# Half-block issue rules and a move of late scaling and sums to VectorE in a fused attention and gated-unit kernel

## The chip, the cores and the metric

The kernel runs on one core of one Trainium2 chip. The metric is the device time of one launch in microseconds (us). The engines are named as the profile names them: PE is TensorE (matmuls; PEld are its weight loads), ACT is ScalarE, DVE is VectorE, POOL is GpSimd, and SP is the engine whose queue issues nearly all transfers.

## The reference

The input is a sequence of 2048 rows of 640 features. It is normalised over the features, and then goes through two branches: full attention with 32 heads of 20 features each, and a gated unit with 1728 hidden features. The result combines the two.

```
xn = layernorm(A_x)
q, k, v = split_heads(xn @ wqkv)              # 32 heads of 20
s = softmax(q k^T * 20**-0.5) v, heads joined, @ wo
g = silu((sigmoid(xn @ w_gate) * (xn @ w_up)) @ w_down)
out = A_x + s * g
```

All arrays are bf16. The exponentials dominate: 32 heads x 2048 x 2048 scores.

## The kernel before

**Blocks.** Attention is cut into 32 blocks: 8 groups of 4 heads times 4 chunks of 512 queries. A block has 64 score tiles (4 heads x 16 key tiles), each 128 keys x 512 queries, one PSUM bank. The last two groups are interleaved (blocks 24 to 31), so block 30 is the last but one, and 31 the last. `base()` is the first block with score tiles not yet claimed, and `n_left[b]` counts them.

**Two ways to an exponential.** A score tile goes either to ScalarE (line 144, `pu<-pst`, two to four banks in one instruction) or to VectorE, where line 1337 turns it to int16 (`iv`) and three passes over four tiles (lines 1040, 1043, 1046, `pb`) build the exponential from its bits. The score matmuls are line 936, and the sums over the keys (PV matmuls) line 988. When a block's PV is complete, `norm_a` copies the sums out (line 1002) and sends the row sums through DRAM, `norm_b` takes the reciprocal (line 1012) and spreads it back (`rl`), and `norm_c` multiplies (line 1025, GpSimd) and stores the scaled block in DRAM (`oD`). Block 30's scaled rows go to an SBUF tile instead (`o6`, line 1029; it appears as `o` in the profile), since the end of the kernel reads it at once.

**Work in between.** Projections and the gated unit (lines 578, 686, 718, 756) are lists of items that fill PE between score fills. `mk_out` items (lines 813 to 825) multiply a finished 128-row tile by `wo`, half a row at a time (h = 0, 1): VectorE multiplies by the gate (line 820) and GpSimd adds the input (line 823); the last sum of a tile is on VectorE once all scores are claimed. `mk_part` items (lines 843 to 851) do the same for the first part of the last four tiles.

**Order.** The order on each engine is written by a planner that runs while the kernel is built: a loop over a clock of 0.01 us which holds a duration for each operation and picks what PE, ACT and DVE issue next. On the chip an engine executes its instructions in that order and waits only for its inputs. The planner's choices are set by 23 numbers (`KEYS`), of which `PLAN` holds one row per block. The ones used below: `wait3` is how long PE waits for a further bank for a wider ScalarE instruction, `third` chooses the banks that may be so used, `four` allows two such banks, `s0` and `dmax` bound how many score tiles VectorE takes per fill, `dl` and `dle` are the numbers of tiles left in a block (`dle` in the last) below which VectorE takes no more, `lag` sets how far the items run ahead.

`gos` is the list of scalings that are ready to be issued: an entry is taken by VectorE's turn from a given time on, as soon as two score tiles wait for VectorE, or 8.0 us (`GO_WAIT`) later at the latest; for odd blocks from 24 (`pressing`) 1.5 us later. VectorE then writes one element (line 1023), which lets GpSimd's multiply start; `pool_at` and `pool_from` keep VectorE's passes in the plan clear of GpSimd. Block 30 was the exception: its multiply was put on GpSimd at once after `norm_b`, with no such signal.

**The end.** After the last PV of block 31 a chain of steps runs: `e_on` (ACT copy), `e_tr` (PE transpose, line 1089), `e_scale` (DVE, lines 786 and 788), `e_back` (PE, line 1098), `e_o` (ACT, line 1102). `early` (line 1076) multiplies `o6` by `wo`, `late_mm` (line 1080) adds block 31, and `tail_steps` combines and stores the last four tiles (lines 1122 to 1136).

Of the kernel before, what the change touches and what calls it, by code (L numbers as in the profile page):

```python
# [14 lines left out]
ALU = mybir.AluOpType  # L15
# [25 lines left out]
            dmax=2, third=4, dord=0, mord=0, mfew=2, npv=4, held=48, burst=1, excl=1, dl=20, dle=8, one=1, four=1, pair=0)  # L41
KEYS = tuple(RULE)
PLAN = (
    (0.25, 4, 0.15, 0.2, 1.8, 0.2, 0.2, 1, 0.0, 2, 4, 0, 5, 2, 3, 48, 1, 1, 20, 8, 1, 1, 0),
    (0.25, 4, 0.15, 0.2, 1.8, 0.2, 0.2, 1, 0.0, 2, 4, 4, 5, 2, 3, 48, 1, 1, 20, 8, 1, 1, 0),
    (0.25, 4, 0.15, 0.2, 1.8, 0.2, 0.2, 1, 0.0, 2, 4, 2, 5, 1, 3, 48, 1, 1, 20, 8, 1, 1, 0),
    (0.25, 5, 0.15, 0, 1.8, 0.2, 0.2, 1, -2.0, 2, 4, 2, 5, 1, 4, 48, 1, 1, 20, 8, 1, 1, 0),
    (0.25, 4, 0.15, 0.2, 1.8, 0.2, 0.2, 1, 0.0, 2, 4, 2, 3, 1, 3, 48, 1, 1, 20, 8, 1, 1, 0),
    (0.25, 5, 0.15, 0, 1.8, 0.2, 0.2, 1, -2.0, 2, 4, 2, 5, 1, 4, 48, 1, 1, 28, 8, 1, 1, 0),
    (0.25, 5, 0.15, 0, 1.8, 0.2, 0.2, 1, -2.0, 2, 4, 2, 3, 1, 4, 48, 0, 1, 20, 8, 1, 1, 0),  # L50
    (0.25, 5, 0.15, 0, 1.8, 0.2, 0.7, 1, 14.0, 2, 4, 2, 3, 1, 4, 48, 0, 1, 20, 8, 1, 1, 0),
    (0.25, 5, 0.15, 0, 0.8, 0.2, 1.0, 1, 14.0, 2, 4, 2, 3, 1, 4, 48, 0, 1, 20, 8, 1, 1, 0),
    (0.25, 4, 0.15, 0.2, 1.8, 0.2, 0.7, 1, 0.0, 2, 4, 0, 0, 2, 4, 48, 1, 1, 20, 8, 1, 1, 0),
    (0.25, 5, 0.15, 0, 0.8, 0.2, 1.0, 1, 14.0, 2, 4, 2, 3, 1, 4, 48, 0, 1, 20, 8, 1, 1, 0),
    (0.25, 5, 0.15, 0, 0.8, 0.2, 1.0, 1, 14.0, 2, 4, 2, 0, 1, 4, 48, 0, 1, 14, 8, 1, 1, 0),
    (0.25, 4, 0.15, 0.2, 1.8, 0.2, 0.7, 1, 0.0, 2, 4, 4, 0, 2, 4, 48, 1, 1, 20, 8, 1, 1, 0),
    (0.25, 5, 0.15, 0, 0.8, 0.2, 1.0, 1, 14.0, 2, 4, 2, 3, 1, 3, 52, 0, 1, 20, 8, 1, 1, 0),
    (0.25, 5, 0, 0, 0.8, 0.2, 1.0, 1, 14.0, 2, 4, 2, 3, 1, 3, 52, 0, 1, 20, 8, 1, 1, 0),
    (0.25, 2, 0.15, 0, 0.8, 0.2, 1.0, 1, 14.0, 2, 2, 2, 5, 1, 3, 52, 0, 1, 20, 8, 1, 1, 0),
    (0.25, 5, 0, 0, 0.8, 0.2, 1.0, 1, 14.0, 2, 3, 2, 3, 1, 3, 52, 0, 1, 20, 8, 1, 1, 0),  # L60
    (0.25, 5, 0, 0, 0.8, 0.2, 1.0, 1, 14.0, 2, 3, 2, 3, 1, 3, 52, 0, 1, 20, 8, 1, 1, 0),
    (0.45, 5, 0, 0, 0.8, 0.2, 1.0, 1, 14.0, 2, 1, 2, 3, 1, 3, 52, 0, 1, 20, 8, 1, 1, 0),
    (0.45, 5, 0, 0, 0.8, 0.2, 1.0, 1, 14.0, 2, 1, 2, 1, 1, 3, 52, 1, 1, 20, 8, 1, 1, 0),
    (0.25, 5, 0, 0, 0.8, 0.2, 1.0, 1, 14.0, 2, 3, 2, 3, 1, 3, 48, 0, 1, 20, 8, 1, 1, 0),
    (0.25, 5, 0, 0, 0.8, 0.2, 1.0, 1, 14.0, 2, 3, 2, 3, 1, 3, 48, 0, 1, 20, 8, 1, 0, 0),
    (0.25, 4, 0, 0, 0.8, 0.2, 1.0, 1, 14.0, 2, 3, 2, 3, 1, 3, 48, 0, 1, 28, 8, 1, 1, 0),
    (0.25, 4, 0, 0, 0.8, 0.2, 1.0, 1, 14.0, 2, 3, 2, 3, 1, 3, 48, 0, 1, 28, 8, 1, 1, 0),
    (0.25, 4, 0, 0, 0.8, 1.2, 1.0, 1, 14.0, 2, 3, 2, 3, 3, 3, 48, 0, 1, 28, 8, 1, 1, 0),
    (0.25, 4, 0, 0, 0.8, 0.2, 1.0, 1, 8.0, 2, 3, 2, 1, 1, 3, 48, 0, 1, 28, 8, 1, 1, 0),
    (0.25, 4, 0.3, 0, 0.8, 0.2, 1.0, 1, 8.0, 2, 3, 2, 1, 1, 3, 48, 0, 1, 28, 8, 1, 1, 0),  # L70
    (0.25, 4, 0, 0, 0.8, 1.2, 1.0, 1, 14.0, 2, 3, 2, 3, 3, 3, 48, 1, 1, 28, 8, 1, 1, 0),
    (0.1, 4, 0, 0, 0.8, 0.2, 1.0, 1, 8.0, 2, 3, 2, 1, 2, 4, 48, 0, 1, 28, 8, 1, 1, 0),
    (0.25, 4, 0.3, 0, 0.8, 1.8, 1.0, 1, 0.0, 2, 3, 2, 1, 2, 4, 48, 0, 1, 28, 8, 1, 1, 0),
    (0.25, 4, 0.3, 0, 0.8, 1.8, 1.0, 1, 0.0, 2, 3, 0, 1, 2, 4, 48, 0, 1, 28, 8, 1, 1, 1),
    (0.25, 4, 0.3, 0, 0.8, 1.8, 1.0, 1, 0.0, 2, 2, 2, 5, 2, 4, 32, 0, 1, 28, 10, 1, 1, 0),
)

PRO = (
# [35 lines left out]
def kernel(  # L114
# [389 lines left out]
    def mark(*e):  # L504
        return lambda t: ev_at.__setitem__(e, t)
# [286 lines left out]
    def load_out(tt):  # L792
# [5 lines left out]
        nc.sync.dma_start(out=out_tiles[tt][1], in_=gq_dram[tt * P:(tt + 1) * P, :])  # L798
        ev_at[("ol", tt)] = now + 4.0

    def pool_hold(t):
        pool_from[0] = max(pool_at[0], t)
        pool_at[0] = pool_from[0] + 0.82

    def mk_out(tt, h, at):
        st = {}

        def alloc():
            st["ps"] = misc_ps()

        def mm(kd):
            hs = slice(h * HD, (h + 1) * HD)
            nc.tensor.matmul(st["ps"][:, 0:HD], lhsT=o_mid[:, kd, tt % 4 * P:(tt % 4 + 1) * P], rhs=wo[kd][:, hs],  # L813
                             start=(kd == 0), stop=(kd == KD - 1))

        def ev():
            xr, gqr = out_tiles[tt]
            sl = slice(h * HD, (h + 1) * HD)
            tmp = w2.tile([P, HD], FP32, tag="gqs", bufs=3, name="otmp")
            nc.vector.scalar_tensor_tensor(out=tmp, in0=st["ps"][:, 0:HD], scalar=0.25,  # L820
                                           in1=gqr[:, sl], op0=ALU.mult, op1=ALU.mult)
            add = nc.vector if h == 1 and claimed[0] == NJOB * NBLK else nc.gpsimd
            add.tensor_tensor(out=xr[:, sl], in0=tmp, in1=xr[:, sl], op=ALU.add)  # L823
            if h == 1:
                nc.sync.dma_start(out=out2[tt * P:(tt + 1) * P, :], in_=xr)
        return Item([("PE", alloc, [(0.136, lambda kd=kd: mm(kd)) for kd in range(KD)]),
                     ("DVE", 0.40, ev, "free", lambda t: (mark("o", tt, h)(t), pool_hold(t)))], at, need=blk(NG - 1, tt // 4),
                    pre=[("oc", tt // 4), ("ol", tt)])


# [189 lines left out]
    def norm_c(b, on, rl, sync):  # L1020
        g, c = gc(b)
        if sync:
            nc.vector.memset(rl[0:1, 0:1], 1.0)  # L1023
        on_bf = w2.tile([P, QC], BF16, tag="on_bf", bufs=2, name="on_bf")
        nc.gpsimd.tensor_tensor(out=on_bf, in0=on, in1=rl, op=ALU.mult)  # L1025
        if b == NBLK - 2:
            last["o6"] = wk.tile([P, QC], BF16, tag="aq", bufs=4, name="o6")[0:GC, :]
            for j in range(GH):
                nc.sync.dma_start(out=last["o6"][j * DH:(j + 1) * DH, :], in_=on_bf[32 * j + 1:32 * j + 1 + DH, :])
            return  # L1030
        for j in range(GH):
            f = g * GC + j * DH
            nc.sync.dma_start(out=oD[f:f + DH, c * QC:(c + 1) * QC], in_=on_bf[32 * j + 1:32 * j + 1 + DH, :])
# [104 lines left out]
    with tc.manual_schedule(engines={ENG.PE, ENG.Activation, ENG.DVE}):  # L1138
# [16 lines left out]
        cur = None  # L1155
        mode = None
        rule = dict(RULE)
        blk_loaded = -1
        active = []
        u_next, k_next, q_next, k_at = 0, PG, PG * NQC, {}  # L1160
        o_next, l_next = 0, 0
# [38 lines left out]

        guard = 0
        chain_at = 1e9
        while chain or items or glu_items or any(it.i < len(it.ops) for it in active):
            guard += 1
            assert guard < 240000, "the issue order does not end"
            bb = base()
            if bb > blk_loaded:
                blk_loaded = bb
                rule.update(zip(KEYS, PLAN[bb]) if bb < len(PLAN) else ())
                g, c = gc(bb)  # L1210
                if c == 0 and g + 1 < NG:
                    if g % 2 == 1:
                        wvs[(g + 1) // 2] = load_wv((g + 1) // 2)
# [49 lines left out]
            for eng in ("ACT", "DVE"):  # L1263
# [15 lines left out]
                if eng == "DVE" and gos and gos[0][0] <= now and (  # L1279
                        sum(x[3] <= now + 0.3 for x in dq) >= 2 or now > gos[0][0] + (1.5 if pressing(gos[0][1]) else GO_WAIT)):  # L1280
                    _, b, on, rl = gos.pop(0)
                    norm_c(b, on, rl, True)
                    free["DVE"] = now + T_GO
                    pool_from[0] = max(pool_at[0], now + T_GO + 0.15)
                    pool_at[0] = pool_from[0] + 1.3
                    o_at[b] = pool_at[0] + 4.0
                    continue
                it = next((e for e in active if e.i < len(e.ops) and e.ops[e.i][0] == eng and e.open(now)), None)
                if it is not None:
                    op = run_item(it, eng)  # L1290
                    if len(op) > 3 and op[3] == "free":
                        flex[it.bank] = free[eng] + EL[eng]
                    continue
                if eng == "ACT":
                    s = slots[nexp % 2]
# [20 lines left out]
                if tm is not None:  # L1316
                    timed.remove(tm)
                    rl = norm_b(*tm[1:3], tm[3])
                    free["DVE"] = now + 0.16
                    if tm[1] == NBLK - 2:  # L1320
                        norm_c(tm[1], tm[2], rl, False)
                        o_at[tm[1]] = now + 11.5
                        ev_at[("o6",)] = now + 9.5
                    else:
                        gos.append((now + (7.0 if pressing(tm[1]) else GO_AT), tm[1], tm[2], rl))
                    continue
                iv_ok = dq and dq[0][3] <= now
                pass_ok = dve_pass and not (now < pool_at[0] and dq and dq[0][3] <= now + 0.2) and dve_pass[0].get("at", 0.0) <= now and (dve_pass[0]["k"] > 0 or buf_free(pb_left, NPB))
# [227 lines left out]
```

## Time and profile before

| | |
|---|---|
| median of 8 runs | 794.59 us (793.39 to 796.48) |
| the profiled execution | 795.5 us, span 793.8 us |
| granted TensorE clock, mean | 0.995 |
| first exponential of attention on ScalarE | 33.24 us after the start of the span |
| last score matmuls | in 774 to 777 us |
| moved by transfers | 62.62 MB, 79 GB/s |

A group line of the profile names the line, the engine, the operation, the tile written and the tiles read with their shapes, then `x` the count; behind the first bar the busy time in us and the mean length of one in ns; behind the second the idle time of the engine just before them and what ended it. ScalarE's instructions overlap in their records (a next one starts before the one before has ended), so the sum of their lengths is more than the busy time. A timeline line begins with start and length in us; x3 behind it means three instructions merged, and brackets hold the idle time before. In a table of windows the busy times are followed by the granted clock, the share of the transfer engines and GB/s.

### The profile page before, as it was taken

Reading aid. Unit: us, or ns where it says so; the run is one execution under the profiler, and the core shown is the slowest. Engines: PE = TensorE matmul, PEld = TensorE weight load, DVE = VectorE, ACT = ScalarE, POOL = GpSimd, SP = SyncE. Lnnn points to the kernel's source line nnn. Section 1 sums busy time; section 2 is a strip of 40 time slices with the busy share of each in tenths; the row PEclk is TensorE's granted clock in tenths of the full one; section 3 lists DMA queues with packets and bytes.
Section 4 is the critical chain, followed back from the end, with each engine's and each line's share of the span. In section 5 each row is a group of like instructions: output and inputs, shape, how many; then the busy total and the mean of one; then the engine's idle time right before and its main releaser. Section 6 shows DMA issues by size and latency. Waiting matters only on the chain.

```text
span 793.8 us, 17201 instructions
## 1 busy us (share of the span) xinstructions
PE 756.6 (95%) x6509; PEld 273.6 (34%) x6509; DVE 771.5 (97%) x1270; ACT 769.7 (97%) x846; POOL 90.5 (11%) x104
## 2 busy tenths in 40 slices
PE   7899999999999999999999999999999999999895
PEld 6532332333333233334333322333332323333332
DVE  8899999999999999999999999999999999999997
ACT  7899999999999999999999999999999999999992
POOL 6100000001000000000000000000000002302354
PEclk9999999999999999999999999999999999999998
DMA  6521221124222133312114333233123322422511
GB/s 169 160 64 48 69 62 49 46 58 102 69 80 66 33 84 102 86 53 56 48 50 112 96 82 81 61 92 114 41 81 92 90 59 66 117 73 84 160 35 64
DMA packets 95876, 62.62 MB, mean 79 GB/s; under 512 B 36388, under 2 KB 89684, under 8 KB 95792
## 3 DMA queue, kind: packets, MB, share of 16 engines
q1 hardware_dynamic: 95504, 61.18, 27.9%
q8 instruction: 51, 0.84, 0.4%
q14 instruction: 33, 0.27, 0.1%
q10 hardware_dynamic: 288, 0.33, 0.1%
HBM read 47.84 MB, written 13.55 MB: 77 GB/s over the span
## 4 chain that ended last, share of the span: by engine, by line
PE 43%; ACT 39%; DVE 10%; issue 5%; DMA 1%; SPq 1%; ACTq 0%; DVEq 0%
ACT pu L144 34%; PE pst L936 14%; PE pst L988 9%; PE pst L718 8%; PE pst L756 5%; PE pst L578 3%; ACT tnh L144 3%; DVE iv L1337 2%; DVE pb L1046 1%; PE pst L813 1%; ACT td L144 1%; DVE pb L1043 1%; DVE pb L1040 1%; DVE otmp L820 1%; SPq L266 1%
## 5 line engine op out<-in xcount | busy, mean ns | idle before, releaser
L144 ACT ACTIVATE pu<-pst 128x1024 bf16<-128x1024 f32 (+2 forms) x706 | 736.6, 1315 | 2.9 <-PE pst L936 2.8
L1337 DVE TENSOR_SCALAR iv<-pst 128x512 int16<-128x512 f32 x491 | 324.8, 682 | 5.0 <-PE pst L936 2.6
L936 PE MATMUL pst<-q,kT 32*128 32x512 bf16 x2048 | 269.0, 383 | 16.4 <-ACT pu L144 10.8
L988 PE MATMUL pst<-pu,v 128*21 128x512 bf16 x1556 | 175.6, 382 | 0.0
L936 PEld LDWEIGHTS <-kT 32*128 32x128 bf16 x2048 | 82.8, 91 | 257.3 <-issue 245.7
L988 PE MATMUL pst<-pb,v 128*21 128x512 bf16 x984 | 153.5, 382 | 1.7 <-DVE pb L1046 1.0
L1046 DVE TENSOR_TENSOR pb<-iv,pb 128x2048 bf16<-128x2048 bf16 x123 | 151.6, 1233 | 0.6
L718 PE MATMUL pst<-xnT,wgu 128*128 128x512 bf16 x520 | 145.6, 384 | 0.9 <-DVE bt L645 0.4
L1025 POOL TENSOR_TENSOR on_bf<-on,rl 128x512 bf16<-128x512 f32 x31 | 40.0, 1291 | 641.8 <-DVE rl L1023 544.8
L1040 DVE TENSOR_SCALAR pb<-iv 128x2048 int16<-128x2048 int16 x123 | 85.3, 694 | 0.1
L1043 DVE TENSOR_SCALAR pb<-iv 128x2048 int16<-128x2048 int16 x123 | 84.4, 686 | 0.0
L756 PE MATMUL pst<-wd,hT 128*128 128x320 bf16 x448 | 83.1, 302 | 0.9 <-DVE iv L1337 0.5
L988 PEld LDWEIGHTS <-v 128*21 128x21 bf16 x2540 | 48.7, 91 | 83.6 <-issue 61.3
L718 PEld LDWEIGHTS <-wgu 128*128 128x128 bf16 x520 | 38.5, 97 | 63.1 <-issue 41.4
L756 PEld LDWEIGHTS <-hT 128*128 128x128 bf16 x448 | 35.9, 97 | 39.7 <-issue 29.5
L144 ACT ACTIVATE tnh<-pst 128x512 bf16<-128x512 f32 (+1 forms) x56 | 45.8, 818 | 0.0
L578 PE MATMUL pst<-xnT,wu 128*128 128x512 bf16 x160 | 45.4, 383 | 0.4 <-DVE iv L1337 0.4
L726 DVE SCALAR_TENSOR_TENSOR hT<-tnh,pst 128x512 bf16<-128x512 bf16 x52 | 35.4, 682 | 1.1 <-ACT tnh L144 0.5
L686 PE MATMUL pst<-wv,xnT 128*128 128x160 bf16 x280 | 26.9, 234 | 0.7 <-DVE iv L1337 0.5
L823 POOL TENSOR_TENSOR xnT<-otmp,xnT 128x320 bf16<-128x320 f32 x19 | 20.7, 1101 | 37.7 <-DVE otmp L820 37.7
L686 PEld LDWEIGHTS <-xnT 128*128 128x128 bf16 x280 | 19.1, 98 | 10.3 <-issue 9.3
L813 PE MATMUL pst<-xnT,v 128*128 128x320 bf16 x120 | 21.7, 301 | 0.3 <-ACT pu L144 0.2
(115 smaller groups left out, 355.7 us busy)
## 6 DMA issues: line engine op xcount, KB each, us to landing
rl<-rd SPq DMA_DIRECT2D x124, 64.0 KB
wgu<-in_B_w_gate_dram SPq DMA_DIRECT2D x24, 320.0 KB
wgu<-in_B_w_up_dram SPq DMA_DIRECT2D x24, 320.0 KB
gq_dram<-gqs SPq DMA_DIRECT2D x24, 160.0 KB
xnT<-gq_dram SPq DMA_DIRECT2D x10, 320.0 KB
xt<-in_A_x_dram SPq DMA_DIRECT2D x16, 160.0 KB
oD<-on_bf SPq DMA_DIRECT2D x120, 20.0 KB
wd<-in_B_w_down_dram SPq DMA_DIRECT2D x1, 2080.0 KB
```

Of the source, the lines that this page charges most:

```text
L144: return nc.scalar.add_instruction(mybir.InstActivation(func=func, name=nc.get_next_instruction_name(), engine=ENG.Activation, ins=[nc.sca ...
L578: nc.tensor.matmul(st["ps"], lhsT=wus[u][:, kd, i, :], rhs=xnT[:, c, kd, :], start=(kd == 0), stop=(kd == KD - 1))
L686: nc.tensor.matmul(st["ps"][:, i * 2 * GC:(i + 1) * 2 * GC], lhsT=xn_tok(tts[i], kd), rhs=wvs[pr][:, kd, :], start=(kd == 0), stop=(kd == ...
L718: nc.tensor.matmul(st[key][0:fs, :], lhsT=w[:, i, kd, ko * P:ko * P + fs], rhs=xnT[:, c, kd, :], start=(kd == 0), stop=(kd == KD - 1))
L756: nc.tensor.matmul(st["ps"][:, 0:HD], lhsT=hT[0:fsz[kf], kf, t4 * P:(t4 + 1) * P], rhs=wd[0:fsz[kf], kf, h * HD:(h + 1) * HD], start=(kf = ...
L936: nc.tensor.matmul(dst, lhsT=kTs[gc(b)[0] % 2][32 * j:32 * j + 32, kt * P:(kt + 1) * P], rhs=qts[b % 3][32 * j:32 * j + 32, :], start=True ...
L988: nc.tensor.matmul(bank[pv_bank[0]][32 * j:32 * j + DH + 1, :], lhsT=lhsT, rhs=u["src"], start=first, stop=last, tile_position=(0, 32 * j) ...
L1025: nc.gpsimd.tensor_tensor(out=on_bf, in0=on, in1=rl, op=ALU.mult)
L1040: nc.vector.tensor_scalar(out=pb[:, 0, :, :].bitcast(I16), in0=iv, scalar1=0x7F80, scalar2=1, op0=ALU.bitwise_and, op1=ALU.bitwise_or)
L1043: nc.vector.tensor_scalar(out=pb[:, 1, :, :].bitcast(I16), in0=iv, scalar1=0x007F, scalar2=0x3F00, op0=ALU.bitwise_and, op1=ALU.bitwise_or)
L1046: nc.vector.tensor_tensor(out=pb[:, 1, :, :], in0=iv.bitcast(BF16), in1=pb[:, 1, :, :], op=ALU.mult)
L1337: nc.vector.tensor_scalar(out=d["iv"][:, j:j + w, :], in0=pst[:, F_POS[bk]:F_POS[bk] + w, :], scalar1=B_OFF, scalar2=0.0, op0=ALU.add, op1 ...
```

## The change

`PLAN` gets a row per half block (64 rows): a block's second row is loaded when half of its 64 score tiles are claimed. All rows are new. In the early blocks `wait3` is 0.4 and 1.0 where it was 0.2, `third` 4 and 2 where it was 4, `four` is 0 in most later rows, `lag` falls from 14 to 8 and less, and in the last rows `dle` is 12 and 16 where it was 10, and `dmax` 1 where it was 2.

Block 30's multiply goes to VectorE, and it goes through `gos`, from 7.0 us after the reciprocal on. The sums of `mk_out` go to VectorE once 32 (h = 1) or 16 (h = 0) score tiles of the last block are left to claim. The planner's loop runs on until `timed` and `gos` are empty.

```
-            add = nc.vector if h == 1 and claimed[0] == NJOB * NBLK else nc.gpsimd
+            st["v"] = n_left[NBLK - 1] <= (NJOB // 2 if h == 1 else NJOB // 4)
+            add = nc.vector if st["v"] else nc.gpsimd
...
+        def done(t):
+            mark("o", tt, h)(t)
+            if st["v"]:
+                late_dve[0] = 0.42
+            else:
+                pool_hold(t)
...
-        nc.gpsimd.tensor_tensor(out=on_bf, in0=on, in1=rl, op=ALU.mult)
+        (nc.gpsimd if sync else nc.vector).tensor_tensor(out=on_bf, in0=on, in1=rl, op=ALU.mult)
...
-        while chain or items or glu_items or any(it.i < len(it.ops) for it in active):
+        while chain or timed or gos or items or glu_items or any(it.i < len(it.ops) for it in active):
...
+            hb = 2 * bb + (n_left[bb] <= NJOB // 2)
+            if hb > half_loaded:
+                half_loaded = hb
+                rule.update(zip(KEYS, PLAN[hb]) if hb < len(PLAN) else ())
...
-                    norm_c(b, on, rl, True)
+                    norm_c(b, on, rl, b < NBLK - 2)
+                    if b == NBLK - 2:
+                        free["DVE"] = max(now, pool_at[0] if pool_from[0] <= now else now) + 0.60
+                        ev_at[("o6",)] = free["DVE"] + 2.5
+                        continue
...
+                    free["DVE"] += late_dve[0]
+                    late_dve[0] = 0.0
...
-                    if tm[1] == NBLK - 2:
-                        norm_c(tm[1], tm[2], rl, False)
-                        o_at[tm[1]] = now + 11.5
-                        ev_at[("o6",)] = now + 9.5
-                    else:
-                        gos.append((now + (7.0 if pressing(tm[1]) else GO_AT), tm[1], tm[2], rl))
+                    gos.append((now + (7.0 if pressing(tm[1]) or tm[1] == NBLK - 2 else GO_AT), tm[1], tm[2], rl))
```

The first and last rows of the new table, and the last of the old:

```
+    (0.25, 4, 0.15, 0.2, 1.2, 0.2, 0.4, 1, 8.0, 2, 4, 4, 0, 2, 4, 48, 1, 1, 20, 8, 1, 1, 0),
...
+    (0.3, 3, 0.15, 0, 1.8, 2.4, 0.7, 1, 0.0, 1, 4, 2, 1, 1, 3, 32, 0, 1, 28, 12, 1, 0, 0),
+    (0.3, 3, 0.15, 0, 1.8, 2.4, 0.7, 1, 0.0, 1, 4, 2, 1, 1, 3, 32, 1, 1, 28, 16, 1, 0, 0),
...
-    (0.25, 4, 0.3, 0, 0.8, 1.8, 1.0, 1, 0.0, 2, 2, 2, 5, 2, 4, 32, 0, 1, 28, 10, 1, 1, 0),
```

The names of the 23 numbers, in order: urgent, rounds, hold, slack, s0, s1, wait3, fall, lag, dmax, third, dord, mord, mfew, npv, held, burst, excl, dl, dle, one, four, pair.

## The prediction

> **What bounds the kernel now.** I read the engine line of the page first, then its groups, then the busy time in two windows (attention loop and tail), then the waits, and at last the order of time around the spot that the diff edits.
>
> ```profile
> PE 756.6 (95%) x6509; PEld 273.6 (34%) x6509; DVE 771.5 (97%) x1270; ACT 769.7 (97%) x846; POOL 90.5 (11%) x104
> ...
> L144 ACT ACTIVATE pu<-pst 128x1024 bf16<-128x1024 f32 (+2 forms) x706 | 736.6, 1315 | 2.9 <-PE pst L936 2.8
> L1337 DVE TENSOR_SCALAR iv<-pst 128x512 int16<-128x512 f32 x491 | 324.8, 682 | 5.0 <-PE pst L936 2.6
> ...
> L1046 DVE TENSOR_TENSOR pb<-iv,pb 128x2048 bf16<-128x2048 bf16 x123 | 151.6, 1233 | 0.6
> ```
>
> ScalarE and VectorE are both at 97%. They share one pool of work: 2048 score tiles are turned into exponentials, 123 x 4 = 492 of them on VectorE and 1556 on ScalarE. A gain on one is worth only what moves across.
>
> ```profile
> 33.00:775.00 742.00, 721.91 (x6169) 249.63 (x6168) 731.55 (x1181) 740.67 (x789) 67.79 (x58) 1.00 0.28 77
> 775.00:794.00 19.00, 9.16 (x72) 4.41 (x69) 13.43 (x22) 3.80 (x5) 7.07 (x7) 0.89 0.19 66
> ```
>
> The columns are window, length, then the busy time of PE, its loads, DVE, ACT and POOL. In the 742 us of the loop ScalarE is idle 1.33 us and VectorE 742 - 731.55 = 10.45 us. After it comes a tail of 19 us with every engine half idle. The granted clock is 1.00, so nothing is to be had there. The two stretches are worked out apart.
>
> **Part 1, the new rule rows.** The 64 half-block rows change no arithmetic: the same matmuls, exponentials and passes are issued in another order, with another split between the two engines. The trace of before cannot show an order that it did not run; I bound it.
>
> What a filled gap is worth: a tile costs VectorE 0.682 us (L1337) plus a quarter of its three passes, (1.233 + 0.694 + 0.686)/4 = 0.653, so 1.335 us; it costs ScalarE 736.6/1556 = 0.473 us. To end t earlier, ScalarE gives up t/0.473 tiles, which cost VectorE 2.82 t, and VectorE too has t less: 3.82 t of its idle time buys t. All 10.45 us would give 2.7 us.
>
> What fewer ScalarE issues are worth: three tiles in one instruction cost less than three in two.
>
> ```profile
> L144 ACT ACTIVATE pu<-pst 128x1024 bf16<-128x1024 f32 x192 | 202.6, 1237 | 1.0 <-PE pst L936 1.0
> L144 ACT ACTIVATE pu<-pst 128x1536 bf16<-128x1536 f32 x43 | 70.8, 1663 | 0.0
> L144 ACT ACTIVATE pu<-pst 128x512 bf16<-128x512 f32 x32 | 24.5, 792 | 0.0
> ...
> L144 ACT ACTIVATE pu<-pst 128x1024 bf16<-128x1024 f32 x164 | 178.1, 1250 | 0.0
> L144 ACT ACTIVATE pu<-pst 128x1536 bf16<-128x1536 f32 x75 | 123.8, 1665 | 0.0
> L144 ACT ACTIVATE pu<-pst 128x512 bf16<-128x512 f32 x3 | 2.0, 681 | 0.0
> ```
>
> The upper three groups are from 33 to 300 us, the lower from 300 to 567 us. With the few 4-wide ones (3 and 1) the early stretch packs 557 tiles in 270 instructions, 2.06 each, the later 560 in 243, 2.30. A bank more adds about 0.42 us (1.653 - 1.231 by the means of the whole run), so 1556 tiles need 657 us and the other 80 of the 736.6 us belong to 706 issues: 0.113 us an issue, an estimate from these rows. At 2.30 the early stretch saves 28 issues, 3.2 us of ScalarE; VectorE hands work back, and by the same exchange 1/1.355 of it shows: 2.3 us. The rows touch this: `wait3`, how long PE waits for a third bank, goes from 0.2 to 0.4 and 1.0 in the early blocks. But `third` falls from 4 to 2 banks there and `four` becomes 0 later, which point the other way.
>
> Bounds for the loop: from below, +1.0 us, as much again as ScalarE's idle time now, if the order fits the chip worse; from above, 2.7 + 2.5 (all stretches at 2.30, 30 issues) = -5.2 us. I take -3.5, beyond the middle, since the early shapes are demonstrably poorer than the later ones and more frequent rows can mend just that.
>
> **Part 2, the scaling of block 30 (L1025).** In the tail these rows matter:
>
> ```profile
> 767.10 0.24 DVE L1012 RECIPROCAL rt<-lt 128x16 f32<-128x16 f32 x1
> ...
> 768.20 1.87 DVE L1337 TENSOR_SCALAR iv<-pst 128x512 int16<-128x512 f32 x3
> ...
> 773.18 1.27 POOL L1025 TENSOR_TENSOR on_bf<-on,rl 128x512 bf16<-128x512 f32 x1 [4.04 <-DMA rl<-rd]
> 773.45 2.09 DVE L1046 TENSOR_TENSOR pb<-iv,pb 128x2048 bf16<-128x2048 bf16 x1
> ...
> 774.48 3.11 SPq L1029 DMA_DIRECT2D o<-on_bf  x4
> ...
> 779.46 0.40 PE L988 MATMUL pst<-pb,v 128*21 128x512 bf16 x4 [1.02 <-DVE pb L1046]
> ...
> 784.10 1.02 PE L1076 MATMUL pst<-wo_t,o 80*128 80x512 bf16 x4 [0.67 <-DVE otmp L820]
> ```
>
> Removed: 1.27 us on GpSimd. It made VectorE's L1046 take 2.09 instead of 1.23 us, 0.86 us. Added on VectorE: one 512-wide multiply, not shown there; nearest are the 0.68 us copy of the same shape (L1002) and, above, the 320-wide sum of 0.49 us scaled by 1.6, 0.78. I take 0.68, so -0.2 us net. [...]
>
> The larger matter is when it runs. GpSimd took it as soon as `rl` landed (773.18). Now it is queued in `gos`: not before 7 us after the reciprocal (774.1), and then only with two score tiles ready for VectorE, or 8 us later still, at 782.1, since block 30 is not `pressing`. VectorE's last score tiles in this trace run at 768.20, and `dle` rises from 10 to 16, which ends them earlier. So I expect the late exit: program order behind the last pass. On the chip it then starts when VectorE is free after that pass, 779.41, and ends at 780.1; four transfers follow on SP (last issue 2.4 us in; a transfer's landing is seen 2.2 us after issue, 767.37 to 769.56): `o6` is there at about 784.9 instead of 779.2. The eight L1076 matmuls run from 783.04 to 785.12 now, held up by banks; they would end at 784.9 + 1.3 = 786.2. Price +1.1 us. If it comes behind the last scaling (L788, ending 782.33), all of it is 2.9 us later: +4.0. In time, as now: 0. Behind it on VectorE stand only the out sums, and they have the 1.18 us idle before 780.58.
>
> **Part 3, the out sums.** Score matmuls count down to 32 left at about 764 and 16 at 769.5. Of the last eight sums five are on GpSimd; the first (767.39) stays, four move: 768.35, 774.42, 781.15, 783.73. Each adds about 0.40 us of VectorE (next start after an L820). The second gives back 0.60 (L1040 at 775.46 took 1.28 instead of 0.68), the last 0.29. Two lie in VectorE's idle time of the tail. I sum to -0.1 us, between -0.4 and +0.9. The output transfers of these tiles leave SP earlier, where nobody waits for them.
>
> **Part 4, the end of the loop.** With `dle` 16 VectorE's passes end nearer to ScalarE's last exponential. PE's 1.02 us wait for `pb` and 0.67 us for `otmp` can go; next in line would be the PV matmuls themselves and the copy. I take half, -0.9, between 0 and -1.7.
>
> **The sum.** -3.5 - 0.2 + 1.1 - 0.1 - 0.9 = -3.6 us. The profiled execution took 795.5 (span 793.8); the median of 8 is 794.59. -3.6 gives 791.9 for that execution and 791.0 for the median, which I forecast.
>
> **Rivals.** *Everything fits:* the rules keep two tiles queued at 774, `o6` is in time, the loop gives its full 5.2 and the tail 1.7: with the 0.3 of parts 2 and 3, -7.2, so 787.4. For it: the early shapes. Against: `dle` 16. *No effect:* the new order trades gaps for gaps, loop and waits together -0.9, eaten by `o6` at +1.1, with the -0.3 of parts 2 and 3: 794.5. For it: ScalarE's 1.33 us of idle leaves little on the face of it. *Slower, the late `o6`:* the scaling is issued behind L788, +4.0 us, the two tail sums stand ahead of it at 0.9, and the loop gains nothing: +4.9, 799.5; with half the loop's gain 797.7. It decides from the point where `o6` lands after 784.1, when the last scaled block is ready for PE. For it: `GO_WAIT` of 8 us and the 10.5 us from the reciprocal to the last exponential. Against: the loop gain has to fail as well.
>
> **Chances.** Forecast case 0.45, with its own range 789 to 793 (loop between -5 and -2); all fits 0.17; no effect 0.17; late `o6` 0.21. A measurement of this kernel tells about 0.2%, 1.6 us, from no change. Faster 0.62, same 0.17, slower 0.21. The range runs from 786.5 to 797.5: it takes in all cases but the upper part of the last.
>
> **What would show it.** Right: fewer than 706 exponentials issued, or VectorE idle below 10 us in the loop; no L1025 on GpSimd after 755 us; L1046 without a 2 us outlier; the waits of L988 and L1076 gone; `o` transfers on SP after 780. Wrong: the new L1025 row at 774 to 776 (the late exit is not taken), ScalarE idle well over 1.3 us in the loop, or a wait of L1076 on the `o` transfer beyond 3 us. The sum is most exposed in the loop's -3.5, which rests on bounds and not on a row.

## The result and the profile after

The changed kernel takes 797.78 us (median of 13 runs, 796.87 to 800.2) beside 794.42 us before (36 runs). The ratio is 1.0040, with a 95% interval of 1.0031 to 1.0049: slower by 3.2 us, against a forecast of 791.0 us. Its profiled execution took 797.41 us, with a span of 795.6. Lines have moved: in the changed kernel 1066 is the scaling (1025 before), 1081, 1084 and 1087 are VectorE's passes (1040, 1043, 1046), 1382 is `iv` (1337), 854, 858 and 860 are the out tiles (820, 823, 825), 1070 the transfers to `o6` (1029), 1117 and 1121 the last products (1076, 1080), 1163 VectorE's first step behind them (1122), 176 ScalarE's exponentials (144), 977 and 1029 the score and PV matmuls (936, 988), 847 the matmuls of the out tiles (813), and 820 the chain's own scaling (788).

The page's engine line and groups, as shown of before, first. The second number behind the bar is the mean in ns.

```profile
PE 759.3 (95%) x6509; PEld 274.4 (34%) x6509; DVE 769.9 (97%) x1276; ACT 768.3 (97%) x830; POOL 82.8 (10%) x99
...
L176 ACT ACTIVATE pu<-pst 128x1024 bf16<-128x1024 f32 (+2 forms) x690 | 735.1, 1330 | 2.2 <-PE pst L977 1.9
L1382 DVE TENSOR_SCALAR iv<-pst 128x512 int16<-128x512 f32 x492 | 324.6, 681 | 5.0 <-PE pst L977 2.8
```

690 exponential instructions instead of 706, with the same split of 1556 and 492 tiles, and less work on GpSimd: the loop moved the way that was hoped. In its windows VectorE is idle 9.9 us (10.45 before). The loss is in the tail, where the granted clock (the number behind the busy times) is 0.68 instead of 0.89.

```profile
33.00:775.00 742.00, 725.03 (x6190) 250.46 (x6188) 732.10 (x1186) 741.47 (x776) 62.65 (x55) 1.00 0.28 77
775.00:796.00 21.00, 8.81 (x54) 4.47 (x49) 11.91 (x23) 1.26 (x3) 4.30 (x4) 0.68 0.17 60
```

ScalarE's timelines give the length of the loop itself: the first line of each is its first run of exponentials, the second its last (start, length). Before:

```profile
30.02 6.52 ACT L144 ACTIVATE pu<-pst 128x1024 bf16<-128x1024 f32 x7 [1.54 <-PE pst L936]
...
755.48 22.15 ACT L144 ACTIVATE pu<-pst 128x1536 bf16<-128x1536 f32 x19
```

After:

```profile
29.54 6.68 ACT L176 ACTIVATE pu<-pst 128x1024 bf16<-128x1024 f32 x6 [1.54 <-PE pst L977]
...
755.90 19.20 ACT L176 ACTIVATE pu<-pst 128x1024 bf16<-128x1024 f32 x20
```

From the first start to the last end it was 777.63 - 30.02 = 747.61 us, and is 775.10 - 29.54 = 745.56 us: 2.05 us shorter. (The 33.24 us in the table of the section on before is the start of the first long piece in the chain of waits, not of the first exponential.) Behind the last exponential the timeline of the changed kernel reads:

```profile
777.93 0.49 DVE L820 TENSOR_TENSOR onq<-pst,rq 128x320 bf16<-128x320 f32 x1
...
779.26 0.68 DVE L1066 TENSOR_TENSOR on_bf<-on,rl 128x512 bf16<-128x512 f32 x1
...
787.20 0.76 DVE L1163 SCALAR_TENSOR_TENSOR hT<-pst,gql 128x256 f32<-128x256 f32 x2 [5.39 <-PE pst L1121]
```

```profile
779.98 3.13 SPq L1070 DMA_DIRECT2D o<-on_bf  x4
```

```profile
778.73 0.98 PE L847 MATMUL pst<-xnT,v 128*128 128x320 bf16 x6
784.44 2.29 PE L1117 MATMUL pst<-wo_t,o 80*128 80x128 bf16 x8 [4.73 <-DMA o<-on_bf]
786.52 2.34 PE L1121 MATMUL pst<-wo_t,o 80*128 80x128 bf16 x8
```

Block 30's scaling is late: it stands behind the chain's own scaling (L820) and starts at 779.26 instead of 773.18, though its inputs are there some 8 us earlier (in o6_pool, below, GpSimd starts on them at 770.70). PE then waits 4.73 us for the transfers, and eight matmuls take 2.29 us where they took 1.25 in other kernels. From the last exponential to VectorE's step behind the products (before: 785.38 - 777.63 = 7.75 us) it is now 787.20 - 775.10 = 12.10 us. This step before:

```profile
785.38 0.75 DVE L1122 SCALAR_TENSOR_TENSOR hT<-pst,gql 128x256 f32<-128x256 f32 x2 [0.52 <-PE pst L1080]
```

### The profile page after: what moved, and what is told of

The parts are those of the page before. It is cut to its first block, busy times and chain, and to the rows that moved or that the text cites. A ratio compares the mean times of both kernels' runs of the same rounds, so it can differ in the third digit from the quotient of the medians.

```text
span 795.6 us, 17147 instructions
## 1 busy us (share of the span) xinstructions
PE 759.3 (95%) x6509; PEld 274.4 (34%) x6509; DVE 769.9 (97%) x1276; ACT 768.3 (97%) x830; POOL 82.8 (10%) x99
## 4 chain that ended last, share of the span: by engine, by line
ACT 52%; PE 34%; DVE 8%; issue 5%; DMA 1%; SPq 0%; ACTq 0%; DVEq 0%
ACT pu L176 45%; PE pst L977 11%; PE pst L750 7%; PE pst L1029 6%; PE pst L788 4%; ACT tnh L176 3%; DVE iv L1382 2%; DVE pb L1087 2%; PE pst L847 2%; PE pst L610 1%; ACT td L176 1%; ACT sq L372 1%; ACT xnT L396 1%; ACT sq L370 1%; PE pst L884 1%
## 5 line engine op out<-in xcount | busy, mean ns | idle before, releaser
L1029 PE MATMUL pst<-pu,v 128*21 128x512 bf16 x1556 | 177.6, 382 | 0.3 <-ACT pu L176 0.2
L1087 DVE TENSOR_TENSOR pb<-iv,pb 128x2048 bf16<-128x2048 bf16 x123 | 151.2, 1229 | 0.5
L750 PE MATMUL pst<-xnT,wgu 128*128 128x512 bf16 x520 | 143.8, 382 | 1.2 <-DVE iv L1382 0.5
L1066 POOL TENSOR_TENSOR on_bf<-on,rl 128x512 bf16<-128x512 f32 x30 | 38.4, 1280 | 633.3 <-DVE rl L1064 560.4
L1043 DVE COPY on<-pst 128x512 f32<-128x512 f32 x31 | 21.1, 682 | 0.3 <-PE pst L1029 0.2
```

The source lines that it names most:

```text
L750: nc.tensor.matmul(st[key][0:fs, :], lhsT=w[:, i, kd, ko * P:ko * P + fs], rhs=xnT[:, c, kd, :], start=(kd == 0), stop=(kd == KD - 1))
L1029: nc.tensor.matmul(bank[pv_bank[0]][32 * j:32 * j + DH + 1, :], lhsT=lhsT, rhs=u["src"], start=first, stop=last, tile_position=(0, 32 * j) ...
L1066: (nc.gpsimd if sync else nc.vector).tensor_tensor(out=on_bf, in0=on, in1=rl, op=ALU.mult)
L1087: nc.vector.tensor_tensor(out=pb[:, 1, :, :], in0=iv.bitcast(BF16), in1=pb[:, 1, :, :], op=ALU.mult)
```

## The experiments

**Theory 1**: the new rules gain, and the late scaling of block 30 takes more than that back. **Theory 2**: the new order of the loop is itself the loss, and the tail would end late anyway. A third, smaller one: the sums on VectorE hold up the chain at the end. Each ratio below is to the kernel before on the same chip; a difference between two ratios takes it that they carry over from chip to chip.

**go_soon: the changed kernel, the scaling's latest time 1.5 instead of 8 us behind its earliest.**

```
-    now > gos[0][0] + (1.5 if pressing(gos[0][1]) else GO_WAIT)
+    now > gos[0][0] + (1.5 if pressing(gos[0][1]) or gos[0][1] == NBLK - 2 else GO_WAIT)
```

> Block 30's scaling stays on VectorE, but it is issued at the latest 1.5 us after its earliest time instead of 8.0 us. Its place in VectorE's order is then between the last passes, some 6 us earlier. Theory 1 (the scaling comes too late for the end, and PE waits for o6 and then runs at half clock): PE's 4.7 us wait for the o transfer goes and the clock stays at 1.0 in the last matmuls; the last matmul ends 5 to 6 us earlier and the time is 791 to 793 us. Theory 2 (the new order of the loop is what costs, and the tail would end late anyway): 797 to 798 us.

Measured: 793.98 us, ratio 0.9988 (0.9978 to 0.9998). The wait of PE for the transfers is gone, and eight products take 1.25 us instead of 2.29, as its PE timeline shows:

```profile
781.69 1.25 PE L1117 MATMUL pst<-wo_t,o 80*128 80x128 bf16 x8
782.78 1.25 PE L1121 MATMUL pst<-wo_t,o 80*128 80x128 bf16 x8
```

Theory 2 falls: the order up to 772 us is the same, and the time is not. But it is 1 to 3 us short of what was expected: the planner also put two more sums of out tiles ahead of VectorE's last pass, which now ends at 777.8 instead of 775.0 us.

**o6_pool: the changed kernel, the scaling back on GpSimd at once after the reciprocal.**

```
-    (nc.gpsimd if sync else nc.vector).tensor_tensor(out=on_bf, in0=on, in1=rl, op=ALU.mult)
+    nc.gpsimd.tensor_tensor(out=on_bf, in0=on, in1=rl, op=ALU.mult)
...
+    if tm[1] == NBLK - 2:
+        norm_c(tm[1], tm[2], rl, False)
+        o_at[tm[1]] = now + 11.5
+        ev_at[("o6",)] = now + 9.5
+    else:
```

> The changed kernel with block 30's scaling back on GpSimd, issued at once after the reciprocal; new rules and sums on VectorE stay. Theory 1: as without the late scaling, 791 to 793 us; VectorE's pass beside the scaling is stretched by some 0.9 us, so it is at most 1 us away from the kernel that issues it sooner. Theory 2: 797 to 798 us.

Measured: 793.32 us, ratio 0.9979 (0.9968 to 0.9990). Between this and the changed kernel lies the whole price of the moved scaling: 1.0040 - 0.9979 = 0.0061, 4.8 us. The distance from the last exponential (775.08) to VectorE's next step says the same from inside: 12.10 - 7.26 = 4.84 us.

```profile
782.34 0.76 DVE L1163 SCALAR_TENSOR_TENSOR hT<-pst,gql 128x256 f32<-128x256 f32 x2 [0.59 <-PE pst L1121]
```

**old_rows: the changed kernel with the 32 old rule rows, each twice.**

```
+    PLAN = tuple(row for row in OLD_PLAN for _ in range(2))
```

> The changed kernel with the 32 old rule rows, each for both halves of its block; the late scaling and the sums on VectorE stay. Theory 1: the late scaling costs here too, with nothing gained in the loop: the last exponential ends at about 777.6 us as before and the time is 797 to 800 us. Theory 2: 794 to 795 us, as before.

Measured: 801.02 us, ratio 1.0075 (1.0060 to 1.0090), 1 us beyond the upper end of what theory 1 said. PE's wait for `o` is 4.60 us and the eight products take 2.29 us here too: the price does not come from the new rules.

```profile
786.59 2.29 PE L1117 MATMUL pst<-wo_t,o 80*128 80x128 bf16 x8 [4.60 <-DMA o<-on_bf]
```

**rows_only: the new rules alone** (the edit of o6_pool, and the old condition for the sums).

```
-    st["v"] = n_left[NBLK - 1] <= (NJOB // 2 if h == 1 else NJOB // 4)
+    st["v"] = h == 1 and claimed[0] == NJOB * NBLK
```

> The kernel with the new rules alone; scaling of block 30 and late sums as before the change. Theory 1: 791 to 793 us, the last exponential ends at about 775.1 us. Theory 2: 797 to 798 us. A third theory, that the sums on VectorE hold up the chain at the end: this one at least 1 us faster than the one that only has the scaling back on GpSimd.

Measured: 792.79 us, ratio 0.9971 (0.9961 to 0.9981), the lowest ratio of all, and faster than both kernels. It gains 2.3 us. In its trace the loop takes 776.23 - 30.87 = 745.36 us, and the tail, last exponential to L1163, 6.57 us instead of 7.75; the first exponential starts 0.85 us later than in the trace of before, which takes part of this back.

```profile
30.87 5.77 ACT L176 ACTIVATE pu<-pst 128x1024 bf16<-128x1024 f32 x5 [1.54 <-PE pst L977]
...
756.17 20.06 ACT L176 ACTIVATE pu<-pst 128x1024 bf16<-128x1024 f32 x21
...
782.80 0.76 DVE L1163 SCALAR_TENSOR_TENSOR hT<-pst,gql 128x256 f32<-128x256 f32 x2 [0.47 <-PE pst L1121]
```

It is not a full 1 us faster than o6_pool, and the intervals overlap, so the third theory is not shown.

**sums_only: old rules, old scaling, the late sums on VectorE** (the rows of old_rows with the edit of o6_pool).

> Old rules, block 30's scaling on GpSimd as before, only the late sums on VectorE. They add 0.4 to 0.5 us each to VectorE, part of it in its idle time, and take away the stretching of one pass: within 0.2% of before, 794 to 796 us. If they hold up the last pass by the sums issued ahead of it: 796 to 797 us.

Measured: 794.96 us, ratio 0.9993 (0.9980 to 1.0005). Under the old rules the sums' move is worth nothing that can be told from zero, either way. Beside old_rows, this run prices the late scaling a second time: 1.0075 - 0.9993 is 6.5 us, and the distance from the last exponential to L1163 is 12.84 us there and 7.84 here, 5.0 us more. The intervals of the two ratios leave room for 1.5 us either way, so this agrees with the 4.8 us within the noise.

**sums_back: go_soon with the old condition for the sums.**

> New rules, block 30's scaling on VectorE issued at the latest 1.5 us after its earliest time, and the late sums as before the change. If the sums on VectorE are what made the kernel with the early scaling only 0.1% faster than before (they stood ahead of VectorE's last pass): about 792.5 us, like the new rules alone. If it is the scaling itself, which stands ahead of that pass too: 793.5 to 794 us.

Measured: 792.87 us, ratio 0.9977 (0.9964 to 0.9989), nearer to 792.5 than to 794. So an early scaling on VectorE is about as good as one on GpSimd (rows_only, 0.9971), and what go_soon lost lay with the sums ahead of the last pass; the intervals of go_soon and sums_back touch, so this is likely rather than settled. Under the new rules the late sums rather cost: with them the ratio is higher by 0.0008 (o6_pool over rows_only) and 0.0011 (go_soon over sums_back), 0.6 and 0.9 us, and the distance from the last exponential to L1163 grows by as much, from 6.57 to 7.26 and from 6.79 to 7.65 us. The ratios alone are within the noise.

**warm_pe: the changed kernel with 18 idle matmuls inside PE's wait**, whose output nothing reads.

```
         tail_banks()
+        for _ in range(18):
+            nc.tensor.matmul(scA[0][:, 0, :], lhsT=ident, rhs=kTs[1][:, 0:512], start=True, stop=True, skip_group_check=True)
```

> The changed kernel with 18 additional matmuls of 512 columns on PE, into a bank that nothing reads any more, between the last projection of the out tiles and the first matmul that needs o6 (some 3.9 us of work inside the 4.7 us wait). Theory 1a (half of the price of the late scaling is the clock that PE loses while it waits): the 16 last matmuls run at the full clock, 2.5 us instead of 4.4, and the time is 1.8 to 2.3 us under the changed kernel's: 795.5 to 796. Theory 1b (the wait for the transfers is the whole price): 797.5 to 798.

Measured: 796.64 us, ratio 1.0024 (1.0015 to 1.0033). The first product that needs the transfers starts as late as before, 9.37 us behind the last exponential (9.34 in the changed kernel), but the sixteen products run at a granted clock of 1.00 (784 to 787 us; 0.50 in the changed kernel), eight in 1.25 us (17 of the 18 idle matmuls are in the records):

```profile
780.66 3.83 PE L1154 MATMUL pst<-kT,ident 128*128 128x512 bf16 x17
785.34 1.25 PE L1117 MATMUL pst<-wo_t,o 80*128 80x128 bf16 x8 [0.84 <-DMA o<-on_bf]
786.42 1.25 PE L1121 MATMUL pst<-wo_t,o 80*128 80x128 bf16 x8
```

So 1.0040 - 1.0024, about 1.3 us, of the 4.8 are the clock, which is 0.50 behind PE's wait; the intervals leave room for 1 us either way. The gain was forecast at 1.8 to 2.3: PE ends 2.06 us earlier relative to the last exponential, but VectorE starts behind the first four products of L1121, only 1.2 us earlier, and from there on VectorE and GpSimd set the pace.

**wait_3 and wait_5: only the scaling's place.** The 8 us of go_soon's edit become 3 or 5; in wait_3 the scaling stands directly behind VectorE's last pass, in wait_5 behind four more instructions of out tiles.

> The changed kernel with the latest time of block 30's scaling 3 us instead of 8 us behind its earliest: it now stands directly behind VectorE's last pass, at about 774.9 us, and everything ahead of it is as in the changed kernel. Theory 1 (only the landing of o6 counts, some 5.2 us behind the start of the scaling, and PE needs it at about 780.4): it lands at about 780.1, no wait of PE, full clock; the chain's own scaling is at most 0.6 us later; 793 to 793.8 us. A rival (any VectorE work between the last exponential and the chain's scaling costs in full): 794 to 795 us.

> The same with 5 us: the scaling stands behind two more out tiles' sums, at about 776.7 us. Theory 1: o6 lands at about 782, PE waits some 1.5 us, and the loss is in between: 794.5 to 795.5 us. If a wait of PE of that length already halves its clock, 796.

Measured: wait_3 792.95 us, ratio 0.9982 (0.9972 to 0.9993); wait_5 794.41 us, ratio 1.0002 (0.9992 to 1.0012). The scaling starts at 775.21 in wait_3, at 777.05 in wait_5 and at 779.26 in the changed kernel; the first matmul that needs it follows 5.40, 5.14 and 5.18 us later. In wait_3 and wait_5 PE is otherwise ready at 780.25 us. With 5.0 us to spare (wait_3) the scaling costs nothing that shows beside o6_pool (0.9979). With 3.2 us to spare (wait_5) PE waits 1.96 us, and the ratio is 0.0020 above wait_3's, 1.6 us; in the changed kernel, where PE is ready 0.45 us behind the start of the scaling, it waits 4.73 us, and the ratio is 0.0058 above wait_3's, 4.6 us. The rival (every VectorE instruction behind the last exponential costs in full) falls with wait_3. In wait_5 the releaser that the profile names for PE's wait is a VectorE sum that ends at 782.13; but in wait_3 the second four of the same products start at 781.67, while that sum (781.66 to 782.15) still runs, so they do not wait for it, and the transfer is left. First wait_3, then wait_5:

```profile
780.61 0.38 PE L1117 MATMUL pst<-wo_t,o 80*128 80x128 bf16 x4 [0.36 <-DMA o<-on_bf]
781.67 1.02 PE L1117 MATMUL pst<-wo_t,o 80*128 80x512 bf16 x4 [0.68 <-DVE otmp L854]
782.54 1.25 PE L1121 MATMUL pst<-wo_t,o 80*128 80x128 bf16 x8
...
782.19 1.25 PE L1117 MATMUL pst<-wo_t,o 80*128 80x128 bf16 x8 [1.96 <-DVE wd L858]
783.27 2.23 PE L1121 MATMUL pst<-wo_t,o 80*128 80x128 bf16 x8
```

**two_queues: the four transfers to `o6` from two queues.**

```
-    nc.sync.dma_start(out=last["o6"][j * DH:(j + 1) * DH, :], ...)
+    (nc.sync if j % 2 else nc.scalar).dma_start(out=last["o6"][j * DH:(j + 1) * DH, :], ...)
```

> The changed kernel with the four transfers to o6 issued alternately from SP and from ScalarE's queue, which is idle then, instead of all four from SP (3.1 us from the first issue to the end of the last). The last one is issued some 1.5 us earlier; PE waits 3.2 us instead of 4.7, and the time is 1 to 1.6 us under the changed kernel's: 796.2 to 796.8 us. If the wait is not made of the issue of these transfers: 797.5 to 798 us.

Measured: 797.81 us, ratio 1.0046 (1.0032 to 1.0061): no gain that shows, and the expectation was wrong. SP's two issues take 1.60 us, and ScalarE's two 2.35; the last ends 2.42 us after the first began instead of 3.13, and PE's wait shrinks from 4.73 to 4.15 us only.

```profile
781.95 2.35 ACTq L1070 DMA_DIRECT2D o<-on_bf  x2
```

**new_from_24: old rules up to block 23, new ones behind, scaling and sums as before.**

> Old rules up to block 23, new ones from block 24 on; scaling and sums as before the change. If the gain of the new rules comes from the first 24 blocks (fewer and wider instructions on ScalarE there): no gain in the loop, 794 to 796 us. If it comes from the end: 792 to 793 us.

Measured: 794.01 us, ratio 0.9984 (0.9976 to 0.9993), the upper of the two answers. Its loop takes 777.50 - 29.82 = 747.68 us, no gain, and the tail 6.31 us. It issues 721 exponentials, 271 of them from 33 to 300 us as under the old rules, where the changed kernel issues 252. So the rules of the first 24 blocks make the loop shorter, and the last ones the tail. Which of the 23 numbers does it was not taken apart (in the first seven blocks `lag` does not fall but rises, from 0 or -2 to 8); the rows act together, since an item that one row puts off has to be done under the next.

## Why the prediction was wrong

The change was forecast at -3.6 us and measured at +3.2. Term by term:

- **The loop, forecast -3.5.** The mechanism, fewer and wider instructions in the early blocks, fits the runs, and the size was twice too large. From the first exponential to the last, the nine profiled kernels with all the new rules take 745.4 to 746.9 us, 746.0 in the mean; the three with the old ones (before, old_rows, sums_only) 746.7 to 748.7, 747.7 in the mean: -1.7 us, though old_rows alone (746.7) lies among the new ones. The early stretch (33 to 300 us), which I had named as poor, went from 2.06 to 2.24 tiles an instruction, not to 2.30:

```profile
L176 ACT ACTIVATE pu<-pst 128x1024 bf16<-128x1024 f32 x183 | 189.2, 1200 | 0.1
L176 ACT ACTIVATE pu<-pst 128x1536 bf16<-128x1536 f32 x60 | 95.9, 1633 | 0.0
...
L176 ACT ACTIVATE pu<-pst 128x2048 bf16<-128x2048 f32 x3 | 6.1, 2049 | 0.0
...
L176 ACT ACTIVATE pu<-pst 128x512 bf16<-128x512 f32 x6 | 4.5, 757 | 0.0
```

  The later stretches were near that already. 16 issues fewer at my 0.113 us, times 0.74 (1/1.355), make 1.3 us, an estimate; VectorE's idle time hardly shrank.
- **The waits at the end, forecast -0.9.** -1.2 us by rows_only (7.75 to 6.57).
- **The late `o6`, forecast +1.1: the step that failed.** The late exit was foreseen, with its cause (`GO_WAIT`, no score tiles left), and so was the time from the start of the scaling to the landing (779.41 to 784.9, 5.5 us; measured 5.1 to 5.4 to the first product). Two things were wrong. First its place: I put it directly behind the last pass, where wait_3 shows it to cost nothing, and kept the place behind the chain's scaling (+4.0) for a rival. The prediction had the planner's latest time, 15 us behind the reciprocal, at 782.1 on the trace of before, where the chain's scaling starts at 781.84; by its own numbers the place was behind it:

```profile
781.84 0.49 DVE L788 TENSOR_TENSOR onq<-pst,rq 128x320 bf16<-128x320 f32 x1
```

  In old_rows, with the old order, it is: the chain's scaling starts at 781.03, block 30's at 781.43. In the changed kernel the reciprocal is at 763.75, so the time is 778.75, and the scaling runs at 779.26. I reasoned about when VectorE would be free instead of what its order would be. Second, a term was left out: behind its 4.73 us of waiting PE ran the sixteen products at a granted clock of 0.50, 1.3 us by warm_pe. Together 4.8 us where the sum had 1.1.
- **The scaling's engine, forecast -0.2, and the sums, -0.1.** The 2.09 us pass is gone (the last three L1087 take 1.21 to 1.23). The 0.29 us of the last sum is from the trace of before, where the sum at 784.08 took 0.78 us and the one at 782.76 0.49; from 772 us on, all seven L858 of the changed kernel take 0.49. A sum costs 0.52 us on VectorE and not 0.40: in the changed kernel the sum at 775.39 starts 0.51 us behind the product that it reads (774.88), where an instruction that does not read the one before follows 0.40 to 0.41 us behind one of this size. In the time neither is clear of noise: sums_only 0.9993; rows_only 0.9971 beside sums_back 0.9977 for the scaling's engine.
- **The second wait, not foreseen.** The tile that takes block 31's scaled result shares its buffer with `rl`, so ScalarE's copy waits for the late multiply as well, for a free buffer and not for an input: it could start when the transposes end, at 778.90, and starts at 780.03, when the multiply has ended (779.94). Here `o6` is later still, and it hides.

With -2.3 (rows_only), +0.6 (from rows_only to o6_pool, not clear of noise) and +4.8 (from there to the changed kernel), the terms add up to +3.1 us; +3.2 was measured. These are steps of one chain of ratios, so that they add up is no proof; the second price of the late scaling, old_rows beside sums_only, is independent of them. The rival "slower, the late `o6`" had the right place but was given 0.21, and the range ended 0.3 us short. That its variant with half the loop's gain, 797.7, met the measured time is in part luck: it left out the clock, and had 0.9 us for the sums.

## What to carry to other kernels

Where a planner writes an engine's order, a deadline in planned time is a place in that order: look up what is issued ahead of it by then, and not when the engine could start. A step that feeds transfers needs its whole chain (here 5.2 us from multiply to use), so move it to a busier engine only with about that much to spare; by wait_3, wait_5 and the changed kernel, 4 us of place decide between nothing and 4.6 us. And when PE has to wait near the end (here 1.96 and 4.73 us), price the work behind the wait at the lower clock too (here 0.50).

## What was not expected of the hardware

The granted clock fell from 1.00 to 0.50 here also while PE was at work. In wait_5 PE's gap is 1.96 us and ends at 782.19; these windows of one us (PE's busy time comes first behind the length) show the clock fall at about 783.4 us, an estimate from the 0.69 in 783 to 784.

```profile
780.00:781.00 1.00, 0.23 (x2) 0.00 (x0) 0.96 (x3) 0.44 (x1) 0.00 (x0) 1.00 0.15 42
781.00:782.00 1.00, 0.00 (x0) 0.00 (x0) 0.97 (x3) 0.00 (x0) 0.00 (x0) 1.00 0.17 56
782.00:783.00 1.00, 0.81 (x7) 0.54 (x8) 0.13 (x1) 0.00 (x0) 0.00 (x0) 1.00 0.36 129
783.00:784.00 1.00, 1.00 (x8) 0.56 (x6) 0.17 (x1) 0.00 (x0) 0.00 (x0) 0.69 0.48 171
784.00:785.00 1.00, 1.00 (x4) 0.29 (x2) 1.00 (x3) 0.00 (x0) 0.60 (x1) 0.50 0.00 0
```

The kernel before shows it in mid-loop: with PE busy 2.19 of the 3 us from 254 to 257, and no gap over 0.63 us, the clock falls at about 257.2 us and is 0.50 until about 260.6, though PE is fully busy from 258 on (estimates from the 0.61 in 257 to 258 and the 0.68 in 260 to 261).

```profile
256.00:257.00 1.00, 0.39 (x3) 0.19 (x3) 1.00 (x3) 1.00 (x3) 0.00 (x0) 1.00 0.84 153
257.00:258.00 1.00, 0.69 (x2) 0.25 (x2) 1.00 (x3) 1.00 (x2) 0.00 (x0) 0.61 0.60 139
258.00:259.00 1.00, 1.00 (x5) 0.10 (x3) 1.00 (x3) 0.59 (x1) 0.00 (x0) 0.50 0.42 139
259.00:260.00 1.00, 1.00 (x5) 0.13 (x2) 1.00 (x2) 0.67 (x1) 0.00 (x0) 0.50 0.07 19
260.00:261.00 1.00, 1.00 (x12) 0.28 (x15) 0.73 (x2) 1.00 (x3) 0.00 (x0) 0.68 0.45 164
```

In the changed kernel PE is idle from 779.71 us, and the clock falls at about 782.7 (an estimate from the 0.85 in 782 to 783), 3.0 us later; it is 0.50 in every window from 783 to 790, while PE is back at work from 784.44 to 788.86. What sets the clock, these traces do not show.
